# Sigmoid attention and a two-layer MLP in float32: a second phase of w_out's product by block products, and what is moved to make room for it

## The chip, the cores and the metric

The kernel runs on one core of one Trainium2 chip. The metric is the device time of one execution in microseconds (us), the median of several runs. The engines are called PE (TensorE), DVE (VectorE), ACT (ScalarE), POOL (GpSimd) and SP (SyncE, which issues nearly all DMAs).

## The reference

```python
scores = scale * np.matmul(q, k.transpose(0, 1, 3, 2)) - np.log(S)   # 8 batches, 12 heads, S = 448, 64
attn = 1.0 / (1.0 + np.exp(-scores))
x = np.matmul(attn, v)             # then heads side by side: x is 3584 x 768
h = x @ w_in                       # w_in 768 x 2048
g = h * np.clip(h + 3.0, 0.0, 6.0) / 6.0
out = g @ w_out                    # w_out 2048 x 768, all float32
```

q, k and v come as float32, the two weights as float64.

## The kernel before

**Numbers.** PE multiplies in fp32r. A float32 operand is split into a high part (an ACT cast to fp32r, line 85) and a low part (a DVE subtraction, line 87), and a product takes three matmuls: high x high, high x low, low x high. The float64 weights arrive as pairs of int32 words, and `decode` turns them into float32 with one ACT and six DVE instructions (lines 66 to 79).

**Attention** takes the first part of the run, 168 steps of four matmul pairs. In its gaps the units `w1_unit` and `w2_unit` (in `todo`, by step number) decode w_in and half of w_out into DRAM.

**w_in.** x @ w_in is done by a scheme of seven block products M1 to M7 (2 x 2 blocks, seven products rather than eight), once for each pair p of batches (4) and quarter of the columns: 16 groups q, 112 slots of 18 matmuls each. `slots` gives their order and `post` what follows a slot: DVE adds the parts from banks A, B and D (tiles cB and cD), gates them to g, forms gT3 and gT2 (`g_sums`), and SP stores all of it to the DRAM tiles gd.

**w_out** is again seven block products, in the order PHASES = M1, M2, M6, M7, M5, M4, M3. Six are "whole": eight units (pair p, half h of the inner dimension) of 36 matmuls each. Each unit needs one moving tile: `g_load` loads gr (896 KB), `g_split` splits it to gx, one to three units ahead. And each half h of a phase needs its stationary weights: `w2_load` loads w2s (768 KB) into a staging buffer, `w2_split` splits it to the three tiles w2_i_h_0 to _2. The last phase, M3, is "fine": for each chunk c of two pairs it applies block products once more. Its items (FINE) are 448-column tiles, blocks B of g and sums T of them, and FINE_PRODUCTS names the weight, the PSUM bank (m_A, m_B, m_D, m_E...) and the output of each block of 12 matmuls: 11 blocks where whole units would have 12. The sums T are made ahead of it on DVE (`pre_load`, `pre_sums`, `pre_store`: tiles pre, then td in DRAM).

**What sets the order.** Each engine runs its instructions in the order in which the program emits them; the dictionaries `on`, `on_late`, `at_slot`, `at_unit`, `at_fetch`, `at_end` attach work to a step, slot or unit. SP is one queue in order, and an instruction that waits for a buffer holds everything behind it. A DMA also waits for the one eight places ahead of it. The pool "stg" has three buffers that the wi, wo, ws and w2s loads take in turn; "ring" has five. In the w_out phase the other half of w_out is decoded by twelve more units, six at units 0 to 5 and six at 8 to 13 (`w2_unit` on DVE, with the DMA wo ahead of it on SP), and `w2_sums` makes the sums of the weight blocks.

Of the kernel before, what the change touches and what calls it, by code (L numbers as in the profile page):

```python
# [8 lines left out]
F32 = mybir.dt.float32  # L9
# [36 lines left out]
FINE = (B11, T1, B21, T2, B12, T3, B22, T4)  # L46
FINE_PRODUCTS = {
    B11: ((A11, "A", True, 0, 0), (E0, "E0", True, None, None)),
    T1: ((S1, "D", True, 1, 1),),
    B21: ((A12, "B", True, 0, 0), (E1, "E0", False, 0, 2)),  # L50
    T2: ((S2, "A", False, 1, 0),),
    B12: ((E0, "E1", True, None, None),),
    T3: ((S3, "A", False, 1, 1),),
    B22: ((S4, "D", False, 1, 0), (E1, "E1", False, 1, 2)),
    T4: ((A22, "A", False, 0, 1),),
# [3 lines left out]
PHASES = (M1, M2, M6, M7, M5, M4, M3)  # L59

# [48 lines left out]
def tile_kernel(ctx: ExitStack, tc: tile.TileContext, qk, vP, wi, wo, outT):  # L109
# [6 lines left out]
    def dram_tile(name, shape):  # L116
# [162 lines left out]
    def w1_unit(j, fh, held):  # L279

        st = staging(f"wi_{j}_{fh}", [P, 2 * KW, 2], I32)
        nc.sync.dma_start(out=st, in_=wi[j, :, fh * 2 * KW : (fh + 1) * 2 * KW])
        yield
        if fh == 0:
            held[j] = ring(f"wA_{j}", [P, 4, KW], F32)
        a = held[j]
        yield from decode(nc, st, a[:, 2 * fh : 2 * fh + 2].rearrange("p k n -> p (k n)"))
        if fh:
            s = ring(f"wS_{j}", [P, 4, KW], F32)
            sums(nc.gpsimd, *(a[:, k] for k in range(4)), *(s[:, k] for k in range(4)))  # L290
            q, r = divmod(j, 2)
            for _ in range(4):
                yield
            nc.sync.dma_start(out=dw1[q][:, :4, r], in_=a)
            nc.sync.dma_start(out=dw1[q][:, 4:, r], in_=s)

    def w2_unit(k, h, ec, held):
# [14 lines left out]
    for u in range(4 * NQ):  # L312
        todo.append((3 + 6 * u, 8, w1_unit(*divmod(u, 2), held)))
# [28 lines left out]
    for n in range(LA):  # L342
        on(NS - 15 + n, w1_load, n)
# [95 lines left out]

    def c22(q, n):  # L440
# [4 lines left out]
    def post(i, q, n):  # L445
        if i == M1:
            copied(q, "s1")
        elif i == M6:
            copied(q, "u2")
        elif i == M7:  # L450
# [14 lines left out]
        elif i == M3:  # L465
# [5 lines left out]
            at_slot(n + 4, store, q, T2)  # L471

# [3 lines left out]

    units = [(i, p, h) for i in PHASES[:-1] for p in range(NPR) for h in range(2)]
    fine = [(c, k) for c in range(NPR // 2) for k in FINE]
    whole, total = len(units), len(units) + len(fine)
    gset, gr, gs, gx = [], {}, {}, {}  # L480

    def g_open():
        gset.append(ctx.enter_context(tc.tile_pool(name=f"g{len(gset)}", bufs=1, reuse_waits="tile")))
# [3 lines left out]
    BLOCK = {B11: (0, 0), B21: (0, 1), B12: (1, 0), B22: (1, 1)}  # L487

    def g_load(n):
        if n < whole:  # L490
            i, p, h = units[n]
            first, _ = PARTS.get(MOVING[i], (MOVING[i], None))
            source = gd[p, first, h]
        else:
            c, k = fine[n - whole]
            if k in BLOCK:
                j, h = BLOCK[k]
                source = gd[2 * c + j, B22, h]
            else:
                source = td[c, k]  # L500
        gr[n] = gset[n % 3].tile([P, FC, S], F32, tag="gr", name=f"gr_{n}")
        nc.sync.dma_start(out=gr[n], in_=source)

    def g_load2(n):
        if n < whole and MOVING[units[n][0]] in PARTS:
            i, p, h = units[n]
            gs[n] = [ring(f"gr_{n}_{k}", [P, 2, S], F32) for k in range(2)]
            for k in range(2):
                nc.sync.dma_start(out=gs[n][k], in_=gd[p, PARTS[MOVING[i]][1], h][:, 2 * k : 2 * k + 2])
# [41 lines left out]
    def w3_sum2():  # L551
        w3s[S2] = w2s[M3, 0][:, 0]
        nc.vector.tensor_tensor(out=w3s[S2], in0=w3s[S1], in1=w3s[S2], op=ALU.subtract)

    def w3_sum4():
        w3s[S4] = w2s[M3, 1][:, 0]
        nc.vector.tensor_tensor(out=w3s[S4], in0=w3s[S4], in1=w3s[S2], op=ALU.subtract)

    def w3_split(tag, *keys):
        gens = []  # L560
        for k in keys:
            if tag == "ring":
# [11 lines left out]
    pre, pre_ctx = {}, ExitStack()  # L574

    def pre_load(c, j):
        if "pool" not in pre:
            pre["pool"] = pre_ctx.enter_context(tc.tile_pool(name="pre", bufs=1, reuse_waits="tile"))
        for k, (e, h) in BLOCK.items():
            pre[k] = pre["pool"].tile([P, 2, S], F32, tag="pre", name=f"pre_{c}_{j}_{k}", bufs=4)  # L580
            nc.sync.dma_start(out=pre[k], in_=gd[2 * c + e, B22, h][:, 2 * j : 2 * j + 2])
# [58 lines left out]
    po_ctx = ExitStack()  # L640
    po_pool = po_ctx.enter_context(
        tc.tile_pool(name="ps_o", bufs=2, space=bass.MemoryType.PSUM, reuse_waits="tile")
    )

    made = {}

    def w2_reload(h):
        for k in (A11, A12):
            held[k, h] = ring(f"w2r_{k}_{h}", [P, EC, FC * P], F32)
            nc.sync.dma_start(out=held[k, h], in_=dw2[k, h])  # L650

    def w2_sums(h):
        a = [held.pop((k, h)) for k in range(4)]
        s1 = ring(f"w2S1_{h}", [P, EC, FC * P], F32)
        nc.vector.tensor_tensor(out=s1, in0=a[A21], in1=a[A22], op=ALU.add)
        nc.vector.tensor_tensor(out=a[A21], in0=a[A11], in1=a[A21], op=ALU.subtract)
        nc.vector.tensor_tensor(out=a[A11], in0=s1, in1=a[A11], op=ALU.subtract)
        made[h] = {A22: a[A22], S1: s1, S2: a[A11], S3: a[A21], S4: a[A12]}
# [52 lines left out]
    xt_close(T1, T4)  # L711
# [4 lines left out]
    acc_ctx = []  # L716
    po, so = {}, {}
# [11 lines left out]
    def out_tile(i, p):  # L729
# [132 lines left out]
```

## Time and profile before

| | us |
|---|---|
| median of 3 runs (lowest, highest) | 1067.1 (1065.45, 1068.09) |
| the profiled execution's own time | 1066.16 |
| its span | 1064.4 |
| PE busy | 1059.2 |
| DVE, ACT, POOL busy | 772.1, 577.9, 39.3 |
| w_in, from first to last slot | 258.33 to 661.73 |
| whole phases of w_out | 661.73 to 1007.17 |
| fine phase M3 | from 1007.17 |

Times are from the start of the span. An engine that is not PE may idle without cost; what counts is whether PE waits. In rows of the profile, "out<-in" gives the tiles without their numbers, L87 is line 87, and a bracket at the end tells how long the engine was idle before the row and what ended that.

### The profile page before, as it was taken

Reading aid. Unit: us, or ns where it says so; the run is one execution under the profiler, and the core shown is the slowest. Engines: PE = TensorE matmul, PEld = TensorE weight load, DVE = VectorE, ACT = ScalarE, POOL = GpSimd, SP = SyncE. Lnnn points to the kernel's source line nnn. Section 1 sums busy time; section 2 is a strip of 40 time slices with the busy share of each in tenths; the row PEclk is TensorE's granted clock in tenths of the full one; section 3 lists DMA queues with packets and bytes.
Section 4 is the critical chain, followed back from the end, with each engine's and each line's share of the span. In section 5 each row is a group of like instructions: output and inputs, shape, how many; then the busy total and the mean of one; then the engine's idle time right before and its main releaser. Section 6 shows DMA issues by size and latency. Waiting matters only on the chain.

```text
span 1064.4 us, 16789 instructions
## 1 busy us (share of the span) xinstructions
PE 1059.2 (100%) x6752; PEld 933.6 (88%) x6752; DVE 772.1 (73%) x801; ACT 577.9 (54%) x623; POOL 39.3 (4%) x38
## 2 busy tenths in 40 slices
PE   9999999999999999999999999999999999999998
PEld 5777777777999999999999999999999999999998
DVE  3679886742578877787787676996876768887685
ACT  6889988886445644664475554434323323232552
POOL 0314230000000000000000000000000000000000
PEclk9999999999999999999999999999999999999999
DMA  8897999782776887688767778869879899888585
GB/s 313 296 327 262 381 362 329 275 313 89 244 249 209 248 305 223 218 268 280 241 212 228 250 236 282 300 268 344 338 299 359 334 344 374 311 336 323 183 288 203
DMA packets 87630, 299.16 MB, mean 281 GB/s; under 512 B 8705, under 2 KB 23297, under 8 KB 87553
## 3 DMA queue, kind: packets, MB, share of 16 engines
q1 hardware_dynamic: 87408, 297.98, 79.1%
q8 instruction: 53, 0.87, 0.3%
q14 instruction: 25, 0.20, 0.1%
q10 hardware_dynamic: 144, 0.11, 0.0%
HBM read 204.60 MB, written 93.45 MB: 280 GB/s over the span
## 4 chain that ended last, share of the span: by engine, by line
PE 97%; DMA 1%; DVE 1%; issue 0%; SPq 0%; DVEq 0%
PE po L771 32%; PE A L401 22%; PE pv L240 12%; PE sc L223 12%; PE D L401 11%; PE B L401 5%; PE m_A L771 1%; PE m_E L771 1%; PE m_D L771 1%; DMA qk<-qk 1%; DMA gr<-gd 1%; DVE gx L87 0%; PE m_B L771 0%; DVE s L721 0%; DVE w L87 0%
## 5 line engine op out<-in xcount | busy, mean ns | idle before, releaser
L771 PE MATMUL po<-gx,w 128*128 128x448 f32 x1728 | 345.8, 362 | 0.0
L771 PEld LDWEIGHTS po<-gx,w 128*128 128x128 f32 x1728 | 324.0, 187 | 21.6
L401 PE MATMUL A<-x,w 128*128 128x448 f32 x1152 | 235.9, 362 | 0.0
L401 PEld LDWEIGHTS A<-x,w 128*128 128x128 f32 x1152 | 215.9, 188 | 15.1 <-issue 0.7
L85 ACT CAST gx<-gr 128x1792 fp32r<-128x1792 f32 x64 | 108.4, 1696 | 167.4 <-PE po L771 133.5
L223 PE MATMUL sc<-qk 64*64 64x448 f32 x1344 | 196.3, 537 | 0.2 <-DMA qk<-qk 0.2
L240 PE MATMUL pv<-a,v 64*64 64x448 f32 x1344 | 195.8, 536 | 0.0
L225 ACT ACTIVATE a<-sc,bias_s 128x896 f32<-128x896 f32 x168 | 168.3, 1011 | 39.9 <-PE sc L223 36.6
L87 DVE TENSOR_TENSOR gx<-gr,gx 128x1792 fp32r<-128x1792 f32 x64 | 129.2, 2019 | 39.7 <-ACT gx L85 39.7
L223 PEld LDWEIGHTS sc<-qk 64*64 64x64 f32 x1344 | 90.5, 134 | 40.1 <-issue 6.2
L240 PEld LDWEIGHTS pv<-a,v 64*64 64x64 f32 x1344 | 93.3, 133 | 34.0 <-issue 3.5
L401 PE MATMUL D<-x,w 128*128 128x448 f32 x576 | 120.4, 362 | 0.0
L87 DVE TENSOR_TENSOR w<-ws,w 128x768 fp32r<-128x768 f32 x112 | 105.8, 951 | 13.9 <-ACT w L85 13.8
L401 PEld LDWEIGHTS D<-x,w 128*128 128x128 f32 x576 | 108.0, 188 | 7.2
L85 ACT CAST w<-ws 128x768 fp32r<-128x768 f32 x112 | 93.0, 830 | 20.6 <-DMA ws<-dw 20.4
L251 DVE TENSOR_TENSOR xr<-pv,y 128x448 f32<-128x448 f32 x48 | 29.9, 622 | 68.4 <-ACT y L250 68.3
L401 PE MATMUL B<-x,w 128*128 128x448 f32 x288 | 60.2, 362 | 0.0
L401 PEld LDWEIGHTS B<-x,w 128*128 128x128 f32 x288 | 54.0, 187 | 3.6
L430 DVE TENSOR_TENSOR cD<-D,u 128x896 f32<-128x896 f32 x32 | 34.8, 1089 | 28.4 <-ACT u L426 20.1
L426 ACT COPY u<-A 128x896 f32<-128x896 f32 x32 | 29.0, 907 | 47.1 <-PE A L401 47.1
L421 ACT ACTIVATE g<-cD,bias 128x896 f32<-128x896 f32 x32 | 33.5, 1046 | 38.7 <-DVE cD L430 38.7
L85 ACT CAST w<-w2s 128x512 fp32r<-128x512 f32 x39 | 23.0, 618 | 45.1 <-DMA w2s<-dw 30.4
(82 smaller groups left out, 804.5 us busy)
## 6 DMA issues: line engine op xcount, KB each, us to landing
gr<-gd SPq DMA_DIRECT2D x56, 896.0 KB, 7.0
ws<-dw SPq DMA_DIRECT2D x112, 384.0 KB, 4.1
gd<-g SPq DMA_DIRECT2D x64, 448.0 KB, 5.0
qk<-qk SPq DMA_DIRECT2D x47, 448.0 KB, 5.8
gd<-gT SPq DMA_DIRECT2D x32, 448.0 KB, 5.4
gr<-gd SPq DMA_DIRECT2D x32, 448.0 KB, 6.3
wi<-wi SPq DMA_DIRECT2D x16, 768.0 KB, 8.0
wo<-wo SPq DMA_DIRECT2D x24, 512.0 KB, 5.3
```

The lines of the kernel that those rows point to most:

```text
L85: nc.scalar.copy(hi, a)
L87: nc.vector.tensor_tensor(out=lo, in0=a, in1=hi.bitcast(F32), op=ALU.subtract)
L223: nc.tensor.matmul(out, k[halves[r], at_k], q[halves[r]], start=True, stop=True)
L225: nc.scalar.activation(a, sc[:, :, :S], AF.Sigmoid, bias=bias_s, scale=scale)
L240: nc.tensor.matmul(pv[p][halves[j], r, :S], v, a[halves[r], int(r != j) if c is None else j], start=first, stop=last)
L251: nc.vector.tensor_tensor(out=xr[b, u][:, k], in0=pv[p][:, 1, :S], in1=y, op=ALU.add)
L401: nc.tensor.matmul(t[:, j, :S], w[:, wk, j, kc], x[:, xk, kc], start=i in (M1, M2, M5) and m == 0, stop=m == 3 * KC - 1, skip_group_check= ...
L421: nc.scalar.activation(r, h, AF.Relu, bias=bias_3, scale=1.0)
L426: nc.scalar.copy(acc[key, q], acc["A", q][:, :, :S])
L430: nc.vector.tensor_tensor(out=c, in0=acc[name, q][:, :, :S], in1=acc[key, q], op=ALU.add)
L771: nc.tensor.matmul(out, w[:, wk, c], x[:, xk, c], start=first and c == 0 and xk == 0 and wk == 0, stop=last and c == FC - 1 and wk == 1, s ...
```

## The change

M6 becomes a fine phase as well (TWICE = M6, M3). FINE has seven items instead of eight: the third output chunk takes E0 x B11 directly and starts its other bank from E0 x T1. The count stays 11 blocks a chunk. The sums that M6 needs are made beside g: for odd pairs, `twin_load` brings the other pair's g sum back, `twin_sums` makes four sums of 128x448 on DVE and `twin_store` stores two tiles. The tiles gd hold both halves h in one, so a store of g writes pieces of half the length. M3's sums (`pre`) move from units 18 to 29 to the units 3 to 8 of M1 and M2 (first chunk) and to the beginning of M7 (second). Of w_out, 15 units are decoded in attention rather than 12, with the sums of its first half, and nine in the w_out phase, one for each of the units 0 to 8. The first w_in load waits for a POOL copy that reads the first sigmoid tile. The first three loads of w_in's phase come three to five steps later. Buffers of the w_out phase are taken from pools that open and close around the fine phases.

```diff
-FINE = (B11, T1, B21, T2, B12, T3, B22, T4)
+FINE = (B11, T1, T2, B21, T3, B22, T4)
 FINE_PRODUCTS = {
-    B11: ((A11, "A", True, 0, 0), (E0, "E0", True, None, None)),
-    T1: ((S1, "D", True, 1, 1),),
...
-    B12: ((E0, "E1", True, None, None),),
...
+    B11: ((A11, "A", True, ((0, 0),)), (E0, "E0", True, ((1, 2),))),
+    T1: ((S1, "D", True, ((1, 1),)), (E0, "E1", True, ())),
+    T2: ((S2, "A", False, ((1, 0),)),),
+    B21: ((A12, "B", True, ((0, 0),)), (E1, "E0", False, ((0, 2),))),
+    T3: ((S3, "A", False, ((1, 1),)),),
+    B22: ((S4, "D", False, ((1, 0),)), (E1, "E1", False, ((1, 2),))),
+    T4: ((A22, "A", False, ((0, 1),)),),
 }
+TWICE = (M6, M3)
...
+        if (j, fh) == (0, 0):
+            nc.gpsimd.tensor_copy(st.bitcast(F32)[:, 0, :1], at[0][:, 0, :1])
         nc.sync.dma_start(out=st, in_=wi[j, :, fh * 2 * KW : (fh + 1) * 2 * KW])
...
-    for u in range(4 * EC):
-        kh, ec = divmod(u, EC)
-        todo.append((99 + 4 * u, 6, w2_unit(*divmod(kh, 2), ec, held)))
+    for u, (k, h) in enumerate(((A11, 1), (A22, 0), (A21, 0), (A11, 0), (A12, 0))):
+        for ec in range(EC):
+            todo.append((97 + 4 * (EC * u + ec), 6, w2_unit(k, h, ec, held)))
...
+    over(on_late, (137, 148, 153, 165), w2_sums(0))
...
-        nc.sync.dma_start(out=gd[p, k, j // 2][:, (j % 2) * 2 : (j % 2) * 2 + 2], in_=quad[q, k])
+        nc.sync.dma_start(out=gd[p, k][:, :, j], in_=quad[q, k])
...
+    def twin_load(q):
+        p, j = divmod(q, NQ)
+        quad[q, "twin"] = temp("v", 3, f"twin_{q}")
+        nc.sync.dma_start(out=quad[q, "twin"], in_=gd[p - 1, T2][:, :, j])
+
+    def twin_sums(q):
+        b1, b2 = quad[q, "twin"], quad[q, T2]
+        t = quad[q, "diff"] = temp("T", 3, f"diff_{q}")
+        nc.vector.tensor_tensor(out=t[:, 1], in0=b2[:, 1], in1=b2[:, 0], op=ALU.subtract)
+        nc.vector.tensor_tensor(out=t[:, 0], in0=b2[:, 0], in1=b1[:, 0], op=ALU.subtract)
+        nc.vector.tensor_tensor(out=b1[:, 0], in0=t[:, 1], in1=b1[:, 0], op=ALU.add)
+        nc.vector.tensor_tensor(out=b1[:, 1], in0=b1[:, 1], in1=b1[:, 0], op=ALU.subtract)
...
+            if q // NQ % 2:
+                at_slot(n + 3, twin_sums, q)
+                at_slot(n + 5, twin_store, q)
...
-    for h, n in ((0, 0), (1, 8)):
-        for e in range(2 * EC):
-            k, ec = divmod(e, EC)
-            u = n + e
-            gen = w2_unit(A21 + k, h, ec, held)
-            at_fetch(u - 2, next, gen, None)
-            over(at_unit, [u, u + 1, u + 1, u + 1, u + 1], gen)
-        at_fetch(n + 4, w2_reload, h)
-        at_unit(n + 2 * EC, w2_sums, h)
...
-    for r in range(NPR):
-        n = 18 + 3 * r
-        at_fetch(n, pre_load, *divmod(r, 2))
-        at_end(n + 1, pre_sums)
...
+    for e in range(3 * EC):
+        k, ec = divmod(e, EC)
+        gen = w2_unit((A12, A21, A22)[k], 1, ec, held)
+        at_fetch(e - 2, next, gen, None)
+        over(at_unit, [e, e + 1, e + 1, e + 1, e + 1], gen)
+    at_unit(4, w2_keep, A12, 1)
+    at_fetch(4, w2_reload, A11, 1)
+    over(at_unit, (10, 10, 11, 11), w2_sums(1))
...
+    for c, n in enumerate((3, begin[M7] + 1)):
...
+        for r in range(2):
+            at_fetch(n + 3 * r, pre_load, c, r)
+            at_end(n + 3 * r + 1, pre_sums)
+            at_fetch(n + 3 * r + 2, pre_store, c, r)
```

Three places in the order of instructions are used below. The first is DVE's order at the end of w_in. Names are tiles with their numbers: cB_15 and cD_15 are group 15's sums read from banks B and D, g0 to g7 its parts of g, gx_0 the first moving tile of w_out. Before:

```order
L430 TENSOR_TENSOR cB_15_6000<-B_15_5981,s1_15_5858 128x896
L87 TENSOR_TENSOR w_111_5973<-ws_111_5923,w_111_5973 128x768
L87 TENSOR_TENSOR gx_0_5975<-gr_0_5920,gx_0_5975 128x1792
L412 SCALAR_TENSOR_TENSOR g0_15_6002<-g0_15_6002,cB_15_6000 128x896
L430 TENSOR_TENSOR cD_15_6034<-D_15_6015,u3_15_5970 128x896
```

After:

```order
L87 TENSOR_TENSOR gx_0_6047<-gr_0_5990,gx_0_6047 128x1792
L478 TENSOR_TENSOR diff_14_6086<-gT2_14_6051 128x448
L479 TENSOR_TENSOR diff_14_6086<-gT2_14_6051,twin_14_5872 128x448
L480 TENSOR_TENSOR twin_14_5872<-diff_14_6086,twin_14_5872 128x448
L481 TENSOR_TENSOR twin_14_5872<-twin_14_5872 128x448
L442 SCALAR_TENSOR_TENSOR g0_15_6074<-g0_15_6074,cB_15_6072 128x896
L460 TENSOR_TENSOR cD_15_6111<-D_15_6092,u3_15_6042 128x896
```

The four twin sums of group 14 now stand between gx_0 and g0_15. Those of group 15 stand in the same way between gx_2 and the first decode.

The second place is SP's order around the loads of M2's weights, w2s_1_0 and w2s_1_1 (wo_k_h_ec is a raw piece of w_out, dw2 a decoded block, gr_n unit n's moving tile). Before:

```order
L525 DMA w2s_1_0_6375<-dw2_1_0_75 128x1536
L502 DMA gr_9_6377<-gd_0_1_1_90 128x1792
L300 DMA wo_2_1_0_6427<-wo 128x1024
L502 DMA gr_10_6429<-gd_1_1_0_101 128x1792
L300 DMA wo_2_1_1_6488<-wo 128x1024
L525 DMA w2s_1_1_6490<-dw2_1_1_76 128x1536
```

After:

```order
L597 DMA w2s_1_0_6483<-dw2_1_0_75 128x1536
L575 DMA gr_9_6485<-gd_0_1_88 128x1792
L300 DMA wo_3_1_2_6535<-wo 128x1024
L656 DMA pre_0_1_0_6537<-gd_0_2_89 128x896
L656 DMA pre_0_1_1_6539<-gd_0_2_89 128x896
L656 DMA pre_0_1_7_6541<-gd_1_2_95 128x896
L656 DMA pre_0_1_2_6543<-gd_1_2_95 128x896
L575 DMA gr_10_6545<-gd_1_1_94 128x1792
L597 DMA w2s_1_1_6602<-dw2_1_1_76 128x1536
```

Four loads of pre tiles now stand between the two. In staging order, w2s_1_0 takes the buffer of wo_2_1_2 (the sixth decode of this phase), wo_3_1_2 that of wo_3_1_0 (the seventh), and w2s_1_1 that of w2s_1_0.

The third is DVE's order at the beginning of M2, where w2_1_h_0 to _2 are the weights that the low parts are made for. Before:

```order
L87 TENSOR_TENSOR w2_1_0_1_6442<-w2s_1_0_6375,w2_1_0_1_6442 128x512
L87 TENSOR_TENSOR gx_8_6448<-gr_8_6326,gx_8_6448 128x1792
L662 TENSOR_TENSOR w2r_1_0_6324<-w2r_1_0_6324,w2r_0_0_6322 128x1536
L87 TENSOR_TENSOR w2_1_0_2_6443<-w2s_1_0_6375,w2_1_0_2_6443 128x512
L87 TENSOR_TENSOR gx_9_6501<-gr_9_6377,gx_9_6501 128x1792
L87 TENSOR_TENSOR w2_1_1_0_6540<-w2s_1_1_6490,w2_1_1_0_6540 128x512
```

After:

```order
L87 TENSOR_TENSOR gx_8_6562<-gr_8_6423,gx_8_6562 128x1792
...
L79 TENSOR_TENSOR w2_3_1_6553<-w2_3_1_6553,wo_3_1_0_6419 128x512
L87 TENSOR_TENSOR w2_1_0_2_6557<-w2s_1_0_6483,w2_1_0_2_6557 128x512
L87 TENSOR_TENSOR gx_9_6615<-gr_9_6485,gx_9_6615 128x1792
L660 TENSOR_TENSOR pre_0_1_2_6543<-pre_0_1_2_6543,pre_0_1_7_6541 128x896
L661 TENSOR_TENSOR pre_0_1_7_6541<-pre_0_1_7_6541,pre_0_1_0_6537 128x896
L662 TENSOR_TENSOR pre_0_1_0_6537<-pre_0_1_2_6543,pre_0_1_0_6537 128x896
L663 TENSOR_TENSOR pre_0_1_1_6539<-pre_0_1_1_6539,pre_0_1_0_6537 128x896
L87 TENSOR_TENSOR w2_1_1_0_6658<-w2s_1_1_6602,w2_1_1_0_6658 128x512
```

Where one w2 sum stood behind gx_8 there is now a whole decode (its last row is shown), and the second set of pre sums stands ahead of the low part of w2_1_1.

More of the change, by code (lines that the diff above doesn't have):

```diff
@@ L475, in x_load @@
         nc.sync.dma_start(out=xr[2 * p + k, u], in_=xd[2 * p + k, u])
[L477 to L483, printed above, removed]
+    items, begin = [], {}
+    for i in PHASES:
+        begin[i] = len(items)
+        if i in TWICE:
+            items += [(i, c, k, True) for c in range(NPR // 2) for k in FINE]
+        else:
+            items += [(i, p, h, False) for p in range(NPR) for h in range(2)]
@@ new lines, in tile_kernel, with g_open, g_tile @@
+    total = len(items)
+    gset, used, gr, gs, gx = {}, {}, {}, {}, {}
+    def g_open(key, *tags, side="left"):
+        stack = ExitStack()
+        pool = stack.enter_context(tc.tile_pool(name=f"g{key}{len(used)}", bufs=1, side=side, reuse_waits="tile"))
+        for tag in tags:
+            gset[tag, key] = pool
+            used[tag, key] = -1
+        return stack
+    def g_tile(tag, n, shape, dtype):
+        spare = ("x",) if tag == "gx" else ("y0", "y1", "y2")
+        keys = [k for t, k in gset if t == tag and (items[n][3] or k not in spare)]
+        key = min(keys, key=lambda k: used[tag, k])
+        used[tag, key] = n
+        return gset[tag, key].tile(shape, dtype, tag=f"{tag}{key}", name=f"{tag}_{n}")
@@ L485, in tile_kernel, with g_shut @@
+    def g_shut(stack, *keys):
+        for key in keys:
+            del gset[key]
+        stack.close()
     PARTS = {T1: (B12, B11), T4: (B21, T2)}
     BLOCK = {B11: (0, 0), B21: (0, 1), B12: (1, 0), B22: (1, 1)}
+    SUM = {T1: (0, 0), T3: (0, 1), T2: (1, 0), T4: (1, 1)}
     def g_load(n):
-        if n < whole:
-            i, p, h = units[n]
+        i, p, k, fine = items[n]
+        if not fine:
             first, _ = PARTS.get(MOVING[i], (MOVING[i], None))
-            source = gd[p, first, h]
-        else:
[L495 to L500, printed above, removed]
@@ L501, in g_load @@
-        gr[n] = gset[n % 3].tile([P, FC, S], F32, tag="gr", name=f"gr_{n}")
+            source = gd[p, first][:, k]
+        elif k in BLOCK:
+            source = gd[2 * p + BLOCK[k][0], MOVING[i]][:, BLOCK[k][1]]
+        else:
+            source = td[i, p, SUM[k][0]][:, SUM[k][1]]
+        gr[n] = g_tile("gr", n, [P, FC, S], F32)
         nc.sync.dma_start(out=gr[n], in_=source)
     def g_load2(n):
-        if n < whole and MOVING[units[n][0]] in PARTS:
-            i, p, h = units[n]
+        if n < total and not items[n][3] and MOVING[items[n][0]] in PARTS:
+            i, p, h, _ = items[n]
@@ L542, in tile_kernel, with w3_sums @@
     w3, w3s = {}, {}
-    def w3_sums():
-        a, b = (w2s[M3, h] for h in range(2))
-        s1 = staging("w3S1", [P, FC * P], F32)
+    def w3_sums(i):
+        a, b = (w2s[i, h] for h in range(2))
+        s1 = staging(f"w3S1_{i}", [P, FC * P], F32)
         nc.vector.tensor_tensor(out=s1, in0=a[:, 1], in1=b[:, 1], op=ALU.add)
@@ L639, in tile_kernel @@
     ps_ctx.close()
[L640 to L658, printed above, removed]
@@ L746, in post2 @@
             eh, k, other = {M2: (0, 0, p), M5: (1, 1, ("u3", p)), M4: (1, 0, ("u3", p))}[i]
-            o = out_tile(i, p)
+            o = keep["low"].tile([P, EC, S], F32, tag="o", name=f"o_{i}_{p}", bufs=2)
             stt(o, t, so[other])
@@ L753, in tile_kernel, with free @@
     next_load, next_split = 4, 2
+    def free(tag, n, top):
+        spare = ("x",) if tag == "gx" else ("y0", "y1", "y2")
+        return min(used[t, k] for t, k in gset if t == tag and (items[n][3] or k not in spare)) < top
     def look_ahead(n):
         nonlocal next_load, next_split
-        while next_load < total and next_load <= n + (4 if n < whole else 5) and next_load - 3 < next_split:
+        fine = items[n][3]
+        near = max((m for m in range(3) if n + 3 - m < total and items[n + 3 - m][3]), default=0)
+        while next_load < total and next_load <= n + (7 if fine else 4 + near) and free("gr", next_load, next_split):
             g_load(next_load)
@@ L762, in look_ahead @@
         g_sum(n + 3)
-        while next_split < total and next_split <= n + (2 if n < whole else 3):
+        while next_split < total and next_split <= n + (3 if fine else 2) and next_split < next_load and free("gx", next_split, n):
             for _ in g_split(next_split):
```

274 lines of the change are left out of this document (168 added, 106 removed).

## The prediction

> **What bounds the kernel now.** I read the page first, then the chain of work that ended last, then the span cut into its four stages.
>
> ```profile
> span 1064.4 us, 16789 instructions
> PE 1059.2 (100%) x6752; PEld 933.6 (88%) x6752; DVE 772.1 (73%) x801; ACT 577.9 (54%) x623; POOL 39.3 (4%) x38
> PE 97%; DMA 1%; DVE 1%; issue 0%; SPq 0%; DVEq 0%
> ```
>
> TensorE (PE) works through 1059.2 of 1064.4 us, and 97% of the chain is PE. So a matmul that goes away saves its whole duration, and nothing that other engines gain can show; what they lose shows as soon as PE waits. By stage (windows: us, then PE, weight loads, DVE, ACT, POOL, granted clock, DMA share, GB/s):
>
> ```profile
> 4.00:258.00 254.00, 253.77 (x2696) 179.40 (x2688) 168.66 (x229) 215.02 (x253) 38.92 (x32) 1.00 0.84 304
> 258.33:661.73 403.40, 403.40 (x2017) 378.19 (x2018) 299.81 (x290) 220.17 (x249) 0.00 (x0) 1.00 0.75 242
> 661.73:1007.17 345.44, 345.44 (x1730) 323.83 (x1728) 262.50 (x244) 117.04 (x104) 0.00 (x0) 1.00 0.84 318
> 1007.17:1061.10 53.93, 53.29 (x265) 49.16 (x263) 40.31 (x35) 24.17 (x15) 0.00 (x0) 1.00 0.72 256
> ```
>
> Attention, w_in and the six whole phases of w_out run without a gap, at clock 1.00. Small holes are at the start and in the fine phase M3; the means of DVE and of the DMA leave room in each stage. The change can lose only where they are full for a while, and two finer windows and the DVE's own rows show where that is:
>
> ```profile
> 665.00:690.00 25.00, 25.00 (x127) 23.43 (x126) 23.06 (x27) 10.69 (x10) 0.00 (x0) 1.00 0.79 290
> 690.00:715.00 25.00, 25.00 (x127) 23.44 (x126) 23.58 (x27) 11.85 (x11) 0.00 (x0) 1.00 0.73 297
> ```
>
> In the first 53 us of w_out DVE is busy for 23.06 and 23.58 of 25 us. It has no place there for more work.
>
> **The change part by part.** The sum stands against the profiled run's own 1066.16 us (1064.4 of span and 1.8 around it); the median of the runs is 1067.1, 0.94 above it. Places are in the clock of the trace before.
>
> *Fewer matmuls.* M6 takes 288 matmuls as eight whole units and 2 chunks x 11 blocks x 12 = 264 as a fine phase: 24 fewer. A matmul takes 0.2 us on the chain in both forms: 345.61 us over 1728 there, 2.40 us from one fine block to the next here.
>
> ```profile
> 661.73 345.61 PE po L771 x1728
> 1019.17 2.56 PE L771 MATMUL m_A<-gx,w 128*128 128x448 f32 x12
> 1021.57 2.56 PE L771 MATMUL m_E<-gx,w_E 128*128 128x448 f32 x12
> 1024.74 2.65 PE L771 MATMUL m_A<-gx,w 128*128 128x448 f32 x12 [0.61 <-DVE s L721]
> ```
>
> That is -4.8 us. The third row begins 0.77 us late, because bank m_A has one block between two of its uses. The new order puts two between them, so I take -0.8; both ends are 0 and -1.1 (53.9 us of stage against 52.8 of blocks). Four more casts and differences for the 28 instead of 24 items cost nothing: ACT has 24.17 of 53.93 us there and DVE 40.31.
>
> *The held first w_in load.* PE waits 1.01 us for the second qk load, which now shares its time with wi:
>
> ```profile
> 2.11 6.40 DMA qk<-qk
> 8.56 0.14 PEld L223 LDWEIGHTS sc<-qk 64*64 64x64 f32 x2 [1.01 <-DMA qk<-qk]
> ```
>
> Held back, wi no longer shares; but SP, in order, stands at it until the first sigmoid tile is there, and the qk loads queued behind it issue some 4 us later. From -1.0 to +1.5; I take -0.5.
>
> *Attention and w_in.* Three more decoded units (3.4 us of DVE each) and four sums of 128x1536 (1.8 each) lie in the second half of attention, 17.3 us in all. Its windows have room for them, the last above all, so they are hidden:
>
> ```profile
> 200.00:225.00 25.00, 25.00 (x272) 18.56 (x268) 16.29 (x29) 20.89 (x27) 0.00 (x0) 1.00 0.80 282
> 225.00:250.00 25.00, 25.00 (x272) 18.58 (x268) 6.19 (x10) 19.37 (x23) 0.00 (x0) 1.00 0.59 210
> 705.00 1.76 DVE L655 TENSOR_TENSOR w2S<-w,w 128x1536 f32<-128x1536 f32 x1
> ```
>
>  The twin sums add 4 x 128x448 to each of eight w_in steps. The nearest row is 622 ns, so 2.5 us per step of 25.2 us; DVE has 299.81 of 403.40 us there, so they are hidden wherever nobody waits soon. 24 loads and stores of 0.46 MB, 11 MB over 403 us, raise 242 GB/s to 269: hidden too. One place is not, the end:
>
> ```profile
> L251 DVE TENSOR_TENSOR xr<-pv,y 128x448 f32<-128x448 f32 x48 | 29.9, 622 | 68.4 <-ACT y L250 68.3
> 652.84 2.02 DVE L87 TENSOR_TENSOR gx<-gr,gx 128x1792 fp32r<-128x1792 f32 x1
> 654.78 1.08 DVE L412 SCALAR_TENSOR_TENSOR g<-g,cB 128x896 f32<-128x896 f32 x1
> 655.78 1.08 DVE L430 TENSOR_TENSOR cD<-D,u 128x896 f32<-128x896 f32 x1
> 657.97 3.76 PE L401 MATMUL D<-x,w 128*128 128x448 f32 x18
> ```
>
> The order puts the sums of step 14 between gx_0 and g0_15. So cD_15, which reads bank D, ends at 656.86 + 2.5 = 659.4, and the last w_in slot, which adds into D, starts at 659.4 instead of 658.0: +1.4 (0 to +2).
>
> *The entry of w_out.* This term decides. From gx_1 on DVE runs one queue: splits of moving tiles (2.02) and decodes (3.44 from first to last row), by turns.
>
> ```profile
> 665.55 2.02 DVE L87 TENSOR_TENSOR gx<-gr,gx 128x1792 fp32r<-128x1792 f32 x1 [2.69 <-ACT gx L85]
> 672.68 0.42 DVE L68 TENSOR_SCALAR w<-w 128x512 f32<-128x512 f32 x1
> 676.12 2.02 DVE L87 TENSOR_TENSOR gx<-gr,gx 128x1792 fp32r<-128x1792 f32 x1
> 682.39 2.02 DVE L87 TENSOR_TENSOR gx<-gr,gx 128x1792 fp32r<-128x1792 f32 x1 [0.81 <-ACT gx L85]
> 694.04 2.02 DVE L87 TENSOR_TENSOR gx<-gr,gx 128x1792 fp32r<-128x1792 f32 x1 [0.80 <-ACT gx L85]
> 704.28 0.69 DVE L79 TENSOR_TENSOR w<-w,wo 128x512 f32<-128x512 f32 x1
> 802.24 1.08 DVE L585 TENSOR_TENSOR pre<-pre,pre 128x896 f32<-128x896 f32 x1
> 806.62 1.55 DVE L721 SCALAR_TENSOR_TENSOR s<-po,s 128x1344 f32<-128x1344 f32 x1
> ```
>
> Before, the sixth decode (last row 704.28) ends at 705.0. After, the queue starts 1.4 later, has the twin sums of step 15 (2.5) and four pre sums (806.62 - 802.24 = 4.4) ahead of that point, and uses up the two gaps of 0.8 us: 711.7. Behind it stood the w2 sums, which go to attention; but now come three further decodes and a second set of pre sums. The loads of M2's weights hang on these decodes, since they take their staging buffers in turn:
>
> ```profile
> 693.26 0.32 SPq L525 DMA_DIRECT2D w2s<-dw  x1
> 715.79 0.32 SPq L525 DMA_DIRECT2D w2s<-dw  x1
> 720.22 1.67 ACT L85 CAST w<-w2s 128x512 fp32r<-128x512 f32 x3 [6.35 <-DMA w2s<-dw]
> 720.87 1.90 DVE L87 TENSOR_TENSOR w<-w2s,w 128x512 fp32r<-128x512 f32 x3 [3.18 <-ACT w L85]
> DMA to landing us min/median/max: 4.4/6.8/12.1
> 785.94 2.19 SPq L581 DMA_DIRECT2D pre<-gd  x4
> 725.00:730.00 5.00, 5.00 (x27) 4.69 (x26) 2.03 (x2) 4.30 (x4) 0.00 (x0) 1.00 1.02 425
> ```
>
> Before, the second load is issued at 715.79 and its low part starts at 720.87; unit 9 needs it at 661.7 + 9 x 7.2 = 726.5, so about 5 us are left. After:
> - w2s_1_0 issues behind the sixth decode, 711.7, lands 5.5 later (between 4.4 and 6.8) at 717.2; two casts (1.1), gx_8's cast (1.7) and its split (2.0) end at 722.0. Unit 8 is due at 661.7 + 57.6 + 1.4 = 720.7 and needs the low part in its second matmul: +1.2 (0 to +2.5).
> - The seventh decode ends at 722.0 + 3.4 = 725.4. SP stands until then at wo_3_1_2; only then follow four pre loads, gr_10, and w2s_1_1 at about 728.9. Ahead of w2s_1_1 and with it are 0.52 + 4 x 0.46 + 0.92 + 0.79 = 4.06 MB. At 425 GB/s, with 2.5 us for a load's own delay (4.4 less 0.79 MB / 425), the pre tiles are there at 733.5 and w2s_1_1 at 737.5.
> - On DVE the second pre sums stand ahead of w2_1_1's low part: 733.5 + 4.4 = 737.9. The cast is there at 738.1, the low part at 738.8, and the third matmul of the unit uses it, so PE starts at 738.4. Due is 720.7 + 1.2 + 7.2 = 729.1: +9.3. Its lower end, 7.2 with nothing at unit 8, has each load land for itself (768 KB in 4.4, 448 KB in 3.6); the upper end, 11.1, has the page's median landing of pre loads:
>
> ```profile
> pre<-gd SPq DMA_DIRECT2D x16, 448.0 KB, 7.5
> ```
>
> [...]
>
> After that nothing is short by my reckoning: M6 as a fine phase moves what M3 moves now, at 256 GB/s and DVE at 40 of 54 us; the later pre sums lie in M7.
>
> Sum: -4.8 - 0.8 - 0.5 + 1.4 + 1.2 + 9.3 = +5.8. 1066.2 + 5.8 = 1072.0 for a run like the profiled one, 1072.9 from the median; I say **1072.5**, slower by 0.5%.
>
> **The rivals.**
> 1. *Loads land each for itself.* Then the entry costs 7.2 rather than 10.5: 1066.2 + 2.5 = 1068.7, or 1069.6 from the median, no measurable change. The min landing of 4.4 speaks for it, the median of 6.8 and the 7.5 of pre loads against. [...]
> 2. *DVE is not behind.* The entry costs nothing when the seventh decode ends by about 715, ten us before my 725.4, so that w2s_1_1 comes as early as before. Then -4.8 - 0.8 - 0.5 + 1.4 = -4.7: 1061.5 to 1062.4, faster. Faster at all needs an entry below 1.5 us. The 5 us left at unit 9 before and the room in the stage's mean (262.50 of 345.44) speak for it; the two full windows against.
> 3. *More waits behind the entry.* M6's items are split while M7's weights are fetched, and PE waits there twice as it did at 1024.74, or the entry goes to its upper ends (+2.5 and +11.1): some +4, 1076 to 1078. M3's few holes now speak against.
>
> **How the numbers follow.** About 0.3%, 3.2 us, can be told from no change. My forecast 0.50 (a tenth of that within 0.3%), the first rival 0.16, the second 0.20, the third 0.14. So faster 0.20, same 0.20, slower 0.60. The range goes from within the second rival, 1062, to above the third, 1079; the likeliest case alone has 1069 to 1076.
>
> **What would show it.** In the trace after: matmuls in 24 fewer, PE idle of about 9 us ahead of w_out's tenth unit with a releaser on DVE's w2 split or ACT's cast, the w2s load issued about 13 us later than now (715.79) and in flight for about 8; one wait of about 1 us at the ninth unit and at the last w_in slot; none in M3. The forecast is wrong if DVE has idle time between its sixth and seventh decode other than for w2s_1_0, or if the second pre sums start before 730.

## The result: 1079.7 us, slower by 1.2%

The changed kernel takes 1079.68 us (1078.62 to 1080.59, 4 runs) against 1066.88 for the kernel before on the same chip: a ratio of 1.012, interval 1.0103 to 1.0138. That is slower, as forecast, but by 12.8 us instead of 5.6, and 0.7 us above the range.

The page after, as far as it answers to the lines shown of before:

```profile
span 1078.8 us, 16857 instructions
PE 1059.8 (98%) x6728; PEld 934.0 (87%) x6728; DVE 808.0 (75%) x862; ACT 584.6 (54%) x630; POOL 41.3 (4%) x39
PEclk9999999999999999999999999997999999999999
PE 93%; DMA 3%; DVE 3%; issue 0%; ACT 0%; SPq 0%; DVEq 0%; ACTq 0%
```

PE has 24 matmuls fewer and is still busy for 0.6 us longer; and one slice of the span has a granted clock of 7, where before had 9 in all. By stage (columns as before: us, PE, weight loads, DVE, ACT, POOL, clock, DMA share, GB/s):

```profile
259.32:664.25 404.93, 403.66 (x2018) 378.13 (x2018) 315.44 (x318) 220.15 (x249) 0.00 (x0) 1.00 0.80 267
664.25:796.59 132.34, 120.88 (x578) 111.62 (x577) 99.39 (x110) 47.13 (x45) 0.00 (x0) 0.94 0.88 329
796.59:849.39 52.80, 52.80 (x266) 49.49 (x265) 43.21 (x40) 26.88 (x20) 0.00 (x0) 1.00 0.67 235
849.39:1022.18 172.79, 172.79 (x865) 161.96 (x864) 126.71 (x105) 52.58 (x45) 0.00 (x0) 1.00 0.83 309
1022.18:1075.15 52.97, 52.97 (x265) 49.30 (x263) 37.86 (x35) 20.79 (x13) 0.00 (x0) 1.00 0.61 235
```

Against before: attention ends 1.0 us later (259.32 for 258.33), w_in takes 1.5 more, M1 and M2 take 132.3 instead of 16 x 7.2 = 115.2 us (+17.1), M6 takes 52.8 instead of 57.6 (-4.8), M7 to M4 the same, M3 1.0 less, the tail behind the last matmul 0.3 more. Together +14.1 of the 14.4 by which the span grew. So the saving came, and nearly all of the loss is ahead of M6.

PE's timeline names each wait in that part (start, us, the matmuls; in the bracket the idle time ahead of them and what ended it):

```profile
250.07 0.98 PE L221 MATMUL sc<-qk 64*64 64x448 f32 x8 [1.59 <-ACT a L223]
660.40 3.85 PE L431 MATMUL D<-x,w 128*128 128x448 f32 x18 [1.27 <-DVE cD L460]
724.98 0.60 PE L861 MATMUL po<-gx,w 128*128 128x448 f32 x1 [3.12 <-ACT gx L85]
727.04 9.57 PE L861 MATMUL po<-gx,w 128*128 128x448 f32 x35 [1.46 <-DVE gx L87]
743.48 53.27 PE L861 MATMUL po<-gx,w 128*128 128x448 f32 x252 [6.87 <-ACT w L85]
```

The last three are w_out's ninth and tenth unit, 11.45 us of waiting. The matmuls behind them are slow as well: 35 take 9.57 us where, at 0.2 us from one to the next and 0.36 for the last (362 ns is the mean length of one in the trace before), 34 x 0.2 + 0.36 = 7.16 would do, and 252 take 53.27 instead of 50.56; with the single one (0.60 for 0.36), 5.4 us more than at full speed. The windows there tell why:

```profile
725.00:730.00 5.00, 3.54 (x9) 2.82 (x10) 4.83 (x7) 2.60 (x3) 0.00 (x0) 0.52 0.00 0
740.00:745.00 5.00, 1.52 (x4) 1.25 (x5) 4.67 (x6) 2.19 (x4) 0.00 (x0) 0.50 1.01 361
745.00:750.00 5.00, 5.00 (x17) 4.45 (x17) 4.83 (x8) 4.39 (x4) 0.00 (x0) 0.59 1.04 424
```

The granted clock is at or near half behind the waits, 0.50 to 0.59 in these windows: 17 matmuls in five busy microseconds, where before had 27.

The queue that made PE wait, on DVE, SP and ACT in order of time:

```profile
701.96 1.09 DVE L660 TENSOR_TENSOR pre<-pre,pre 128x896 f32<-128x896 f32 x1 [2.77 <-DMA pre<-gd]
714.56 0.69 DVE L79 TENSOR_TENSOR w<-w,wo 128x512 f32<-128x512 f32 x1
715.28 0.32 SPq L597 DMA_DIRECT2D w2s<-dw  x1
722.20 1.14 ACT L85 CAST w<-w2s 128x512 fp32r<-128x512 f32 x2 [12.84 <-DMA w2s<-dw]
729.74 0.69 DVE L79 TENSOR_TENSOR w<-w,wo 128x512 f32<-128x512 f32 x1
730.46 0.33 SPq L300 DMA_DIRECT2D wo<-wo  x1
730.89 2.11 SPq L656 DMA_DIRECT2D pre<-gd  x4
733.59 0.38 SPq L597 DMA_DIRECT2D w2s<-dw  x1
742.81 1.66 ACT L85 CAST w<-w2s 128x512 fp32r<-128x512 f32 x3 [15.21 <-DMA w2s<-dw]
743.46 1.90 DVE L87 TENSOR_TENSOR w<-w2s,w 128x512 fp32r<-128x512 f32 x3 [0.26 <-ACT w L85]
```

The sixth decode ends at 715.2 and releases w2s_1_0, which is there 6.9 us later; the seventh ends at 730.4, SP issues wo, four pre loads, gr_10 and then w2s_1_1, which is there 9.1 us after its issue. The chain is the one that the prediction named, but later. Three things in it the prediction did not have: DVE standing 2.77 us for the first pre loads (the first row here), the clock, and the first row of PE's: at the end of attention ACT stood 2.44 us for the first load of w_in's weights, and the sigmoid tile behind it came late to PE.

```profile
238.29 1.66 SPq L352 DMA_DIRECT2D ws<-dw  x2
248.28 0.83 ACT L85 CAST w<-ws 128x768 fp32r<-128x768 f32 x1 [2.44 <-DMA ws<-dw]
```

### The profile page after: what moved, and what is told of

Same layout as the page of the kernel before. It is cut to its first block, busy times and chain, and to the rows that moved or that the text cites. A ratio compares the mean times of both kernels' runs of the same rounds, so it can differ in the third digit from the quotient of the medians.

```text
span 1078.8 us, 16857 instructions
## 1 busy us (share of the span) xinstructions
PE 1059.8 (98%) x6728; PEld 934.0 (87%) x6728; DVE 808.0 (75%) x862; ACT 584.6 (54%) x630; POOL 41.3 (4%) x39
## 4 chain that ended last, share of the span: by engine, by line
PE 93%; DMA 3%; DVE 3%; issue 0%; ACT 0%; SPq 0%; DVEq 0%; ACTq 0%
PE po L861 24%; PE A L431 21%; PE sc L221 11%; PE pv L238 11%; PE D L431 10%; PE B L431 5%; PE m_A L861 4%; PE m_E L861 4%; PE m_D L861 2%; DMA ws<-dw 1%; PE m_B L861 1%; DMA w2s<-dw 1%; DMA pre<-gd 1%; DMA gr<-gd 1%; DVE gx L87 1%
## 5 line engine op out<-in xcount | busy, mean ns | idle before, releaser
L861 PE MATMUL po<-gx,w 128*128 128x448 f32 x1440 | 294.2, 366 | 11.5 <-ACT w L85 6.9
L861 PEld LDWEIGHTS po<-gx,w 128*128 128x128 f32 x1440 | 273.7, 190 | 31.6 <-ACT w L85 7.2
L85 ACT CAST gx<-gr 128x1792 fp32r<-128x1792 f32 x68 | 115.0, 1696 | 169.1 <-PE po L861 106.0
L221 PE MATMUL sc<-qk 64*64 64x448 f32 x1344 | 189.1, 538 | 1.6 <-ACT a L223 1.6
L238 PE MATMUL pv<-a,v 64*64 64x448 f32 x1344 | 188.6, 536 | 0.0
L87 DVE TENSOR_TENSOR gx<-gr,gx 128x1792 fp32r<-128x1792 f32 x68 | 137.3, 2022 | 30.6 <-ACT gx L85 30.6
```

The source lines that it names most:

```text
L85: nc.scalar.copy(hi, a)
L87: nc.vector.tensor_tensor(out=lo, in0=a, in1=hi.bitcast(F32), op=ALU.subtract)
L221: nc.tensor.matmul(out, k[halves[r], at_k], q[halves[r]], start=True, stop=True)
L238: nc.tensor.matmul(pv[p][halves[j], r, :S], v, a[halves[r], int(r != j) if c is None else j], start=first, stop=last)
L861: nc.tensor.matmul(out, w[:, wk, c], x[:, xk, c], start=first and c == 0 and xk == 0 and wk == 0, stop=last and c == FC - 1 and wk == 1, s ...
```

## The experiments

**Taking the pre work out of the entry.**

```diff
-    for c, n in enumerate((3, begin[M7] + 1)):
+    for c, n in enumerate((begin[M7] + 1, begin[M5] + 1)):
```

> The changed kernel with one number pair altered: the sums for M3's first chunk (pre loads, sums and stores) begin one unit into M7 instead of at unit 3, those for the second chunk one unit into M5. Theory Q (the queue at the entry of w_out): without the two sets of pre loads and sums (4.4 us of DVE each, plus 2.77 us in which DVE stood for the first set's loads) the sixth decode ends about 7 us earlier, w2s_1_0 and w2s_1_1 are issued near 708 and 722, and the waits at the ninth and tenth unit (3.12 + 1.46 and 6.87 us) are gone or below 2 us together; the 5.4 us that PE lost to a lower clock go with them: 1062 to 1065 us, granted clock 1.000. Rival D (nine decodes back to back are too much by themselves): about 5 of 11.5 us of waiting stay, with the lower clock: 1069 to 1073. Rival P (the clock is lower there for another reason than the waits): the waits go and the clock stays near 0.99: 1068.

Measured: 1069.67 us (1067.65 to 1070.52), 1.0024 of before (1.0005 to 1.0043): most of the change's loss is gone, but the time is 5 us above the 1062 to 1065 of theory Q and falls into the 1069 to 1073 of rival D, so the trace has to decide. PE's waits:

```profile
728.74 51.00 PE L861 MATMUL po<-gx,w 128*128 128x448 f32 x252 [0.81 <-ACT w L85]
951.33 59.08 PE L861 MATMUL po<-gx,w 128*128 128x448 f32 x287 [3.38 <-DVE gx L87]
```

At the entry 0.81 us is left of 11.45, the clock there stays at 1.00, and M6 begins at 779.58 instead of 796.59. So theory Q holds for that place. Rival D (the decodes alone, with some 5 us of waiting left there) and rival P (another cause of the lower clock) fall. But the work that was moved makes a new wait at the first unit of M4, where it now meets M5's transfers; DVE stands 6.50 us for a gr load inside M5:

```profile
934.79 2.09 DVE L587 TENSOR_TENSOR gr<-gr,gr 128x896 f32<-128x896 f32 x2 [6.50 <-DMA gr<-gd]
890.00:947.00 57.00, 57.00 (x287) 53.44 (x286) 46.01 (x39) 13.96 (x11) 0.00 (x0) 1.00 0.99 381
```

**The clock by itself.** In the kernel before, PE is made to wait once at w_out's tenth unit, by k passes over M2's second weights that alter no value; nothing else in the program's order moves.

```diff
         st, gens = w2s.pop((i, h)), []
+        for _ in range(5 if (i, h) == (M2, 1) else 0):
+            nc.vector.tensor_tensor(out=st, in0=st, in1=st, op=ALU.max)
```

> The kernel before, with five DVE passes of 1.76 us (a maximum of a tile with itself, which alters no value) over the second weights of M2 ahead of their split, so that PE alone waits, once, at w_out's tenth unit. From the rows of before: landed 720.2, + 8.8, cast 0.6, low part 0.7, needed at 726.9: a wait of 3.4 us. Wait alone: 1066.9 + 3.4 = 1070.3. Theory C (after a wait the clock stays low for a fixed time, 2.5 us lost a wait): 1072.8, with the granted clock near 0.5 for about 5 us behind the wait. Rival (loss in proportion to the wait, 5.4 of 11.45 us): 1071.9.

> As the last one, with eight passes: 14.1 us, a wait of 8.7 us. Wait alone: 1075.6. Theory C, 2.5 us a wait whatever its length: 1078.1. Loss in proportion to the wait: 1079.7.

> The kernel before with four passes over M2's second weights (five gave a wait of 3.28 us, eight one of 8.63). Expected wait 1.5 to 1.7 us. If every wait costs the clock 2.5 us: 1066 + 1.6 + 2.5 = 1070. If only a wait of some 3 us does: 1067.5, with clock 1.000.

Measured, one run each: 1072.67, 1077.69 and 1067.55 us, against 1065.85 and 1065.76 for before. For four, five and eight passes, PE's timeline and the window behind the wait:

```profile
727.50 32.80 PE L773 MATMUL po<-gx,w 128*128 128x448 f32 x161 [1.42 <-ACT w L85]
730.00:735.00 5.00, 5.00 (x27) 4.68 (x26) 3.08 (x4) 4.55 (x5) 0.00 (x0) 1.00 0.90 247
```

```profile
729.50 282.92 PE L773 MATMUL po<-gx,w 128*128 128x448 f32 x1404 [3.28 <-ACT w L85]
730.00:735.00 5.00, 4.96 (x17) 4.34 (x17) 2.53 (x4) 5.00 (x6) 0.00 (x0) 0.66 0.49 154
```

```profile
734.92 282.71 PE L773 MATMUL po<-gx,w 128*128 128x448 f32 x1404 [8.63 <-ACT w L85]
735.00:740.00 5.00, 5.00 (x17) 4.37 (x18) 2.53 (x4) 5.00 (x7) 0.00 (x0) 0.65 0.42 126
```

1404 matmuls at 0.2 us take 280.96. So the wait of 3.28 us cost 2.0 more behind it, the one of 8.63 us 1.8 more, and the one of 1.42 us 0.4 with the clock at 1.00 throughout (the high part comes first, and the low part follows within the unit). By the windows, PE runs at half clock for 3.4 us behind the wait with five passes (a mean of 0.66 from 730 to 735, and 1.00 in the five us before and after) and for 3.6 us with eight (from PE's start at 734.92 to 738.5, as the mean is 0.50 from 730 to 735 and 0.65 from 735 to 740); half of that, 1.7 and 1.8 us, is nearly all of the loss. The loss does not grow with the wait, which refutes the loss in proportion, and it was less than the 2.5 that I had expected. The times agree roughly: with five passes the kernel takes 1072.67 - 1065.85 = 6.8 us longer, of which 3.28 + 2.0 are named above and 1.1 come from M3's waits, which are 1.83 in this run (1.34 and 0.49) and 0.7 before.

**The load or the sums.** Which of the two held w2_1_1 at the tenth unit?

```diff
-            at_end(n + 3 * r + 1, pre_sums)
-            at_fetch(n + 3 * r + 2, pre_store, c, r)
+            at_end(n + 3 * r + 1 + (c == 0 and r == 1), pre_sums)
+            at_fetch(n + 3 * r + 2 + (c == 0 and r == 1), pre_store, c, r)
```

> The changed kernel with the second set of pre sums one unit later on DVE, behind the low parts of w2_1_1; its loads stay ahead of w2s_1_1 on SP. Theory L (the wait at the tenth unit is the load's): the cast of w2_1_1 began at 742.81, as its load landed, and the sums ended at 743.2, so 0.3 to 0.5 us are won: 1079 to 1080, and the wait is 6.4 us. Rival S (the sums on DVE hold the low part, as the prediction's timetable has it, 4.4 us): the wait falls by 2 us or more: 1075 to 1077.5.

Measured: 1080.02 us, one run. The wait is 7.49 us, no shorter than 6.87:

```profile
743.15 16.89 PE L861 MATMUL po<-gx,w 128*128 128x448 f32 x73 [7.49 <-ACT w L85]
```

With the sums behind the weights nothing is gained: the load sets the wait (theory L), and rival S falls. The prediction's timetable had the load's cast last as well, but by a margin of only 0.2 us (cast there at 738.1, sums ended at 737.9); in the changed kernel the sums ended at 743.20, and the low part that follows the cast began at 743.46.

**The held first load.**

```diff
-        if (j, fh) == (0, 0):
-            nc.gpsimd.tensor_copy(st.bitcast(F32)[:, 0, :1], at[0][:, 0, :1])
```

> The changed kernel without the POOL copy that holds the first w_in load. If the hold is worth what the prediction has: PE waits about 1 us for a qk load near 8.5 us again, attention ends 0.5 to 0.8 us later, 1080.3 us. If it is worth nothing: the start is as in the changed kernel, 1079.7.

Measured: 1080.55 us, one run; the time is within what single runs differ by, so the trace decides:

```profile
8.42 0.14 PEld L221 LDWEIGHTS sc<-qk 64*64 64x64 f32 x2 [0.72 <-DMA qk<-qk]
```

The wait for the second qk load is back. Attention's PE work, less its one wait at 250 (1.21 here, 1.59 in the change), ends 0.7 us later (259.63 - 1.21 against 259.32 - 1.59). That is near the 0.5 of the prediction, but one trace against one does not settle it. In the other five kernels here with the hold, attention, less the same wait, ends between 257.4 and 258.4; in the kernel before and the four built on it, all without the hold, between 257.9 and 258.4, and three of these (with four passes, with five, and the next one below) show no wait for that load.

**The order of the fine items alone,** in the kernel before:

```diff
-FINE = (B11, T1, B21, T2, B12, T3, B22, T4)
+FINE = (B11, T1, T2, B21, T3, B22, T4)
...
-    B11: ((A11, "A", True, 0, 0), (E0, "E0", True, None, None)),
-    T1: ((S1, "D", True, 1, 1),),
+    B11: ((A11, "A", True, 0, 0), (E0, "E0", True, 1, 2)),
+    T1: ((S1, "D", True, 1, 1), (E0, "E1", True, None, None)),
...
-    B12: ((E0, "E1", True, None, None),),
```

> The kernel before with only the new order of the fine items and products in M3 (seven items; the third chunk's banks begun at B11 and T1). Theory (bank m_A has two other blocks between two uses): M3's 22 blocks take 52.8 instead of 53.9 us, no wait for DVE's s: 1065.8 us. Rival (the wait is for the split of the moving tile queued on DVE, whatever the order): 53.5 to 53.9 us stay, 1066.9.

Measured: 1065.47 us, one run, and the 22 blocks without a hole. First and last:

```profile
1007.24 2.56 PE L770 MATMUL m_A<-gx,w 128*128 128x448 f32 x12
1057.64 2.57 PE L770 MATMUL m_A<-gx,w 128*128 128x448 f32 x12
```

1057.64 + 2.4 - 1007.24 = 52.8 us, without a wait: that for s was one of spacing, and the new order and products alone remove it.

**Putting the pieces right, in three steps.**

```diff
-    for s, ks in ((138, (A22,)), (150, (S3,)), (155, (S1, S2)), (167, (S4,))):
+    for s, ks in ((138, (A22,)), (150, (S3,)), (158, (S1, S2)), (167, (S4,))):
...
-                at_slot(n + 3, twin_sums, q)
+                at_slot(n + (4 if q == 14 else 3), twin_sums, q)
```

> The changed kernel with three moves: the pre work as in the kernel above; the stores of two weight sums (S1, S2) three attention steps later, so that the first two loads of w_in's weights stand ahead of them on SP; and the twin sums of group 14 one slot later, behind cD_15 on DVE. Theory: 1079.7 - 17 (entry waits and clock) - 1.6 (ACT's and PE's wait for ws_0 at 250) - 1.4 (the last w_in slot) = 1059 to 1062, faster than before by 0.5 to 0.7%. If the entry's waits come mainly from the decodes: 1066 to 1070.

Measured: 1070.48 us (1068.89 to 1070.76), 1.0035 of before (1.0021 to 1.005): not the 1059 to 1062 expected. Both small moves worked: the waits at 250 and in the last w_in slot are gone, and w_out begins at 660.8 instead of 664.25 (663.1 in the first experiment). None of it reached the end, as M6 begins at 779.58, by chance to the hundredth as in the first experiment: w2s_1_1 comes 1.6 us earlier than there and PE 2.4, so PE waits longer, and this time with the clock at half for 3 us (0.50 from 729 to 732), which costs the 1.6 us again; and M4's wait is there as well (3.95 us).

```profile
727.15 52.59 PE L861 MATMUL po<-gx,w 128*128 128x448 f32 x252 [1.58 <-ACT w L85]
```

The next kernel moves that load to the front and the pre work away from M5.

```diff
-    for c, n in enumerate((begin[M7] + 1, begin[M5] + 1)):
+    for c, n in enumerate((begin[M7], begin[M7] + 6)):
...
-        at_fetch(e - 2, next, gen, None)
+        at_fetch(e - (1 if e == 8 else 2), next, gen, None)
...
-                at_fetch(n - 3 + 2 * h, w2_load, i, h)
+                at_fetch(n - 3 + (1 if i == M2 else 2) * h, w2_load, i, h)
```

> The joined kernel with two more moves. The pre work begins at the first unit of M7 (first chunk) and at its seventh (second chunk), so that three of its four sets are in M7 and one in M5: in the two kernels before, with two sets in M5, the DMA share from 890 to 947 was 0.99 and PE waited 3.38 and 3.95 us at M4's first unit. And w2s_1_1 is issued ahead of wo_3_1_2 and gr_10, right behind the seventh decode. Theory: no wait at w_out's tenth unit (1.58 us and a lower clock for 5 us there in the joined kernel), none at M4's entry: 1070.5 - 3.6 - 6.6 = 1060 to 1061. If one set in M5 is still too much for the transfers: a wait of 1 to 3 us at M4 stays, with 0 to 2.5 us of clock: 1062 to 1066.

Measured: 1066.24 us (1063.79 to 1066.5, 10 runs), 0.9999 of before (0.9989 to 1.0009): the same, not the 1060 to 1061 of the theory. The entry is cured, 576 matmuls in one piece; but M5 still waits:

```profile
660.76 115.36 PE L861 MATMUL po<-gx,w 128*128 128x448 f32 x576
896.77 37.87 PE L861 MATMUL po<-gx,w 128*128 128x448 f32 x179 [2.65 <-DVE w L87]
936.12 72.07 PE L861 MATMUL po<-gx,w 128*128 128x448 f32 x359 [1.49 <-DVE gx L87]
```

So one set of pre work in M5 was enough to make PE wait, in M5 itself and not at M4 as expected. M4 has more room than M5 in the changed kernel, so the second chunk's work went there:

```diff
-    for c, n in enumerate((begin[M7], begin[M7] + 6)):
+    for c, n in enumerate((begin[M7] + 1, begin[M4] - 1)):
...
-        at_fetch(n - 5, swap, None, (), "x", g_open, "x", "gx")
+        at_fetch(n - (5 if i == M6 else 3), swap, None, (), "x", g_open, "x", "gx")
```

> The kernel of the last timed run with the pre work moved once more: first chunk from M7's second unit, second chunk from the last unit of M5 on, so that its sums lie in M4 (in the changed kernel M4 has a DMA share of 0.70 and DVE 40.6 of 58 us busy; M5 has 0.94 and 47.7), and M3's extra moving buffer two units later to make room. Theory: M5 and M4 run without a wait, the entry stays cured: 1059 to 1061, faster than before by 0.5%. If M4's transfers are now too many (256 GB/s + 7.3 MB in 58 us = 383 GB/s): a wait of 1 to 4 us at M3's or M4's entry: 1062 to 1066.

Measured: 1062.32 us (1061.17 to 1063.09, 6 runs), 0.9962 of before (0.9949 to 0.9974). This version beats both, by 3.4 us (before, on the same chip) and 17 us. It is above the 1059 to 1061 of the theory and at the low end of the other case, too many transfers in M4. From its views:

```profile
span 1060.9 us, 16863 instructions
989.92 14.48 PE L861 MATMUL po<-gx,w 128*128 128x448 f32 x71 [1.72 <-DVE gx L87]
```

One wait of 1.72 us is left in M4, where the transfers are near full, and the clock is at 1.00 in each stage:

```profile
943.00:1001.00 58.00, 56.28 (x281) 52.41 (x281) 45.95 (x41) 18.52 (x18) 0.00 (x0) 1.00 0.97 368
```

## Why the prediction was wrong

The direction and the place were right, and four of the sum's terms with them:
- *24 fewer matmuls*, -4.8: measured -4.8 (52.80 against 57.6).
- *M3's holes*, -0.8: -1.0 in the changed kernel; the order of the items alone brings the 22 blocks from 53.9 to 52.8.
- *The held load*, -0.5: -0.7 in one pair of traces, which does not settle its size.
- *The last w_in slot*, +1.4: a wait of 1.27 us, 1.5 in the stage.
- *The ninth unit*, +1.2: 3.12 + 1.46 = 4.6. This term was mis-sized. The entry's queue on DVE began 1.1 us later than I had it, as attention ended late; DVE stood 2.77 us for the first pre loads, a wait that I had not looked for; and w2s_1_0, issued right behind the four stores of the first pre sums, took 6.9 rather than 5.5 us.
- *The tenth unit*, +9.3: 6.87. The load came 5.3 us later than in my timetable (742.8 for 737.5), but PE was later still (736.6 for 729.1), through the ninth unit and the clock. From 733.59 to 742.81, while the load was in flight, the transfers ran at 407 GB/s, near the 425 that I had taken.

The two waits together were 11.45 us, against 10.5 forecast, but that is luck: the first was 3.4 us longer, the second 2.4 us shorter because PE came to it late. What counts for the end is when the tenth unit could start, and how fast PE ran behind it.

The first step that failed is the timetable of the loads at w_out's entry. It put DVE's wait for the first pre loads at nothing and had the sixth decode end at 711.7; it ended at 715.2, and with the longer flight of w2s_1_0 each later step came about 5 us late. So the tenth unit started at 743.48 instead of 738.4. About 1.1 of these 5.1 us are the late begin of w_out, the other 4 lie in the entry itself. That the pre work is the cause, the first experiment shows: without it 0.81 us of waiting is left there.

The second step that failed is the charge for a wait. The sum took each wait at its own length, with the clock at 1.00 as in all of the quoted windows. PE lost 5.4 us more behind the two waits, and single waits put into the kernel before show that this comes from the waiting itself. By the rows, only half of the 5.4 reached the end: the 2.7 us behind the ninth unit's waits passed while w2s_1_1 was not there yet (its chain, shown above, runs over DVE and SP, not over PE), and PE would have waited for it instead; the 2.7 us behind the tenth unit's add to the time. This split is worked out; no run separates the two.

The clock fell to 0.50 behind the waits, and came back 3.6 us after PE had begun again with eight passes (734.92 to 738.5) and 5.6 us after at the tenth unit of the changed kernel (743.48 to 749.07). Single waits of 8.63, 3.28, 2.65 and once 1.58 us lowered it. Of my two terms the one of 9.3 us is longer than all of these and the one of 1.2 shorter; at the 2 us measured for one wait, the forecast would have been 1074.5, still 5 us short.

The third failed step is "attention: hidden". It read DVE and ACT by the mean of a window, and left out what a moved step does on SP. The new weight-sum stores stand ahead of the first w_in loads there, which came later too. The first was in flight for 10.0 us, ACT stood behind it with sigmoid tiles in its queue, and PE waited 1.59 us. The same instructions gave waits of 0.47 to 1.21 us in three other kernels, so the size varies from run to run; with the stores behind the loads the wait is gone.

The profiled run is 14.4 us longer than before, against 5.8 in the sum. Of these 8.6 us, about 1.6 were there when w_out began (nearly all from attention), 4 lie in the timetable of the entry, 2.7 in the lower clock behind the tenth unit, and 0.3 in small terms.

Of the rivals the third, 1076 to 1078, came nearest in time, but not for its reasons: M6 ran without a hole, M7's weights were never late, and the two waits were not at their upper ends (4.6 is above the 2.5 given for the ninth unit, 6.87 below even the lower end of 7.2 for the tenth). The first (each load lands for itself) is refuted by 6.9 and 9.1 us in flight, the second by a seventh decode that ended at 730.4 instead of 715.

## What to carry to other kernels

Where PE is the bound, a wait of a few microseconds can cost more than its length: here about 1.7 us more for a single one, and 2.7 behind each of the two places in the changed kernel. It was paid at each of the two, so count the waits and not only their sum; it does not show in the time where PE would have had to wait for a later arrival anyway. When work is moved off one stage, follow each of its loads and stores through the in-order queues of the stage that it goes to. Here the same pre sums, with their loads and stores, made PE wait at the entry of w_out, at M4 and in M5; they cost nothing in M7 (second chunk of the changed kernel) and 1.72 us in M4, where the transfers were near full. And a gain upstream is worth nothing if the next fixed arrival, here one load of weights, does not come earlier with it.

## What the runs showed of the hardware that I had not expected

The loss did not grow with the length of the wait: 3.28 us cost 2.0 and 8.63 us cost 1.8. Among the short waits the length alone did not settle whether it comes: those of 1.42 and 1.72 us left the clock at 1.00, and behind one of 1.49 us 359 matmuls took 72.07 us, 0.1 more than 358 x 0.2 + 0.36; but one of 1.58 us in the joined kernel had it at 0.50 from about 729 to 732, and one of 2.65 us (M5, in the kernel after the joined one) cost 1.9 us more, with a mean clock of 0.97 from 886 to 943.

The traces show one thing more. In the changed kernel the clock goes to 0.50 at 725.18, back to 1.00 at 732.00, down again at 738.83 and back at 749.07: 6.82, 6.83 and 10.24 us from one change to the next, twice, twice and three times the same 3.41 us. Other stretches at half clock, read from the means of windows, last about 3.4 us (five passes, as above; the joined kernel, 728.6 to 732.1; the first experiment, 951.0 to 954.4) and 10.3 us (eight passes, 728.2 to 738.5). What sets these lengths was not shown. In the changed kernel PE was busy for 0.29 and 1.20 of the 3.41 us just ahead of the two drops. The clock came back behind 3.41 us in which PE was busy throughout (728.59 to 732.00 and 745.66 to 749.07); it stayed at 0.50 behind 1.95 us of work (725.18 to 728.59), none (738.83 to 742.24) and 2.18 (742.24 to 745.66). How much idle time lowers it, and how much work brings it back, stays open.
